# Layer norm of u: statistics merged on Pool, one ScalarE pass per row block, modulation of two row blocks per VectorE instruction

## The chip, the cores and the metric

The kernel runs on one core of a Trainium2 chip. The metric is the device time of one execution in microseconds (us), taken as the median of several executions. A core has five engines that each run their own instructions in order and wait for one another by semaphores: TensorE (PE in the profile, with PEld for its weight loads), VectorE (DVE), ScalarE (ACT), Pool (POOL, also called GpSimd) and SyncE (SP), which here only issues transfers. SBUF is the on-chip memory with 128 partitions; PSUM holds TensorE's results.

## What is computed

The reference is one transformer-like block over a sequence of 2048 positions with 512 channels: an adaptively modulated layer norm, a long convolution (S4), and then a second modulated layer norm with a mixer and an MLP. The part around the change is this:

```python
mod = (_silu(c) @ w_mod).reshape(c.shape[0], 6, 1, -1)
sa, ca, ga, sb, cb, gb = (mod[:, 0], ..., mod[:, 5])
h = _layernorm(x, axis=-1) * (1 + ca) + sa      # x is u: 2048 x 512
x = x + ga * _A_ref(h, ...)                     # S4: K = sum_n C exp(dt A l) dt B, FFT convolution of h with K
...
def _layernorm(x, axis=-1, eps=1e-5):
    m = jnp.mean(x, axis=axis, keepdims=True)
    v = jnp.var(x, axis=axis, keepdims=True)
    return (x - m) / jnp.sqrt(v + eps)
```

Each of the 2048 rows of u is normalised over its 512 channels, multiplied by (1 + ca) and shifted by sa; both are multiplied by ga ahead of time, since ga scales the whole branch. The result goes into the Fourier transform of u.

## The kernel before, in words

The program has stages. First come preparations (0 to 39 us of the trace): discretising A, B and C, and the first three parts of the modulation. Then comes the stage that matters here, the generation of the S4 kernel (about 39 to 212 us), a loop of 33 steps (line 553) written out by hand under a manual schedule: every engine runs its instructions in the order of the program text. After it come the two-dimensional spectra and their products (212 to 335 us) and the mixer with the MLP (335 to 715 us).

One step k of the loop issues, in this order:

- the evictions that the step before left in the list `later` (ScalarE): kernel blocks `KX<-kp` after every odd step, Fourier blocks of u `vs<-pu`, and at some steps parts of the modulation (`wm`, `modg`).
- `turns(k + 2)` (line 448): TensorE computes phases into PSUM (`xx`, two buffers), ScalarE takes a sine and a cosine of 128x1024 each into the tile `tr` (three buffers). So phases and sines are made two steps ahead of their use.
- at every fourth step (k = 1, 5, 9, 13, 17, 21, 25; `fresh`, line 561) the exponentials for the next four steps: `exps` (line 243) on TensorE and ScalarE. ScalarE then runs a table load for Exp, five Exp instructions `p<-xx`, and at the end, at line 579, a tiny sine `turn<-hpi` that brings the table load for Sin forward. These steps are called exponential steps below.
- `products(k)` (line 468) on VectorE: two scalar_tensor_tensor of 128x512 (L475), at even k one tensor_tensor of 128x1024 for two steps together (L481), and two tensor_tensor of 128x1024 (L484, L485). All read two tensors from SBUF and write the tiles `e0` and `e1`. In step 0 and at the end of every step with k % 4 == 3 a small `weigh` (L263) is added.
- `burst(k)` (line 499): 64 small matmuls on TensorE from `e0` and `e1`.
- the entries of `side[k]` (lines 515 to 533): the work on u and on the modulation, spread over the steps by a table.

The work on u has 16 row blocks of 128 rows (one row per partition) and 512 channels, four to a tile `xu`. For row block i the table uses at(i) = 1 + (i * 28) // 16, that is 1, 2, 4, 6, 8, 9, 11, 13, 15, 16, 18, 20, 22, 23, 25, 27:

- at side[at(i) - 2] `u_stats` (line 418, through `ln_stats`, line 141): VectorE's bn_stats (L146) and bn_aggr (L147) give mean and variance; Pool adds eps (L149) and takes the power -0.5 (L150).
- at side[at(i)] `u_norm` (line 421): two scalar_tensor_tensor of 128x512 on VectorE, in place: (x - mean) * mods[1] (L424), then x * rstd + mods[0] (L425).
- for every odd i, at side[at(i) + 1] and side[at(i) + 2], `u_dft` (line 427) for the pair of row blocks i - 1 and i: eight matmuls, and for the next step's evictions two ScalarE copies `vs<-pu` and four transfers out on SyncE's queue.

Pool's queue holds, beside these, the issues of eight DRAM-to-DRAM copies of the weights (L519, at side[4], side[7], ... side[25]).

Where the engine instructions stand in the loop, in the lines that matter most:

```python
fresh = k % 4 == 1 and k < 28
if fresh:
    exps(k // 4 + 1, 0, 2)
e = products(k)
...
    act(turn1, hpi, AF.Sin)
...
for f in side[k]:
    f()
```

So what `side[k]` puts on ScalarE in an exponential step stands behind all five Exp instructions and both table loads of that step.

Of the kernel before, what the change touches and what calls it, by code (L numbers as in the profile page):

```python
# [7 lines left out]
F32 = mybir.dt.float32  # L8
F32R = mybir.dt.float32r
I32 = mybir.dt.int32  # L10
AF = mybir.ActivationFunctionType
OP = mybir.AluOpType
# [94 lines left out]
def dram(t, off, ap):  # L107
    return bass.AP(tensor=t.tensor, offset=t.offset + off, ap=ap)


def body(ctx, tc, A):
    nc = tc.nc
    V, S, P, T, Y = nc.vector, nc.scalar, nc.gpsimd, nc.tensor, nc.sync
    pool = lambda name, bufs=1, **k: tc.tile_pool(name=name, bufs=bufs, **k)
    glob = ctx.enter_context(pool("glob"))
    dpool = ctx.enter_context(pool("dscr", space=DRAM))

    def act(out, in_, f=AF.Copy, scale=1.0, bias=0.0):
        return S.activation(out, in_, f, bias=bias, scale=scale)  # L119
# [11 lines left out]
    eps_t = glob.tile([128, 8], F32, name="eps_t")  # L131
    V.memset(eps_t, 1e-5)
    pw = glob.tile([128, 8], F32, name="pw")
    V.memset(pw, -0.5)
    m_one = glob.tile([128, 8], F32, name="m_one")
    V.memset(m_one, -1.0)
    mv1 = glob.tile([128, 16, 2], F32, name="mv1")
    rs1 = glob.tile([128, 16], F32, name="rs1")
    st1 = glob.tile([128, 10, 2, 6], F32, name="st1")

    def ln_stats(pl, xs, tag):
        n = len(xs)
        st = pl.tile([128, n, 6], F32, name=tag + "s")
        mv = pl.tile([128, n, 2], F32, name=tag + "m")
        for i, x in enumerate(xs):
            V.bn_stats(st[:, i], x)  # L146
            V.bn_aggr(mv[:, i], st[:, i])  # L147
        r = pl.tile([128, n], F32, name=tag + "r")
        P.tensor_tensor(r, mv[:, :, 1], eps_t[:, :n], op=OP.add)  # L149
        P.tensor_tensor(r, r, pw[:, :n], op=OP.pow)  # L150
        return mv, r

    def exp_exact(pl, x, shape, name, scale=1.0):
        t = lambda s, dt=F32: pl.tile(shape, dt, name=f"{name}_{s}")
# [47 lines left out]
    mods = [modu[:, k] for k in range(3)] + [modg[:, k] for k in range(3)]  # L202
# [29 lines left out]
    ut = {}  # L232

    def load_u(g):
        x = ut[g] = up.tile([128, 4, 512], F32, name="xu")
        for bp in range(4):
            Y.dma_start(x[bp * 32:(bp + 1) * 32],
                        dram(A["u"], (bp * 16 + g * 4) * 512, [[64 * 512, 32], [1, 2048]]))
# [45 lines left out]
    with tc.manual_schedule():  # L284
# [89 lines left out]
        at, at0 = tmp("at"), tmp("at0")  # L374
# [36 lines left out]
    wk = a1.enter_context(pool("wk", bufs=2, reuse_waits="tile"))  # L411
# [4 lines left out]
    ul = {}  # L416

    def u_stats(b):
        ul[b] = ln_stats(wk, [ut[b // 4][:, b % 4]], "lu")

    def u_norm(b):
        x = ut[b // 4][:, b % 4]
        mv, r = ul.pop(b)
        V.scalar_tensor_tensor(x, x, mv[:, 0, 0:1], mods[1], op0=OP.subtract, op1=OP.mult)  # L424
        V.scalar_tensor_tensor(x, x, r[:, 0:1], mods[0], op0=OP.mult, op1=OP.add)  # L425

    def u_dft(b, cp2):
        x = ut[b // 4]
        ps = [psu.tile([128, 512], F32, name="pu") for h in range(2)]
        for i in range(2):  # L430
            for h in range(2):
                q = 64 * (1 - i if h == 0 else i)
                j = slice(32 * JB[2 * h + cp2], 32 * JB[2 * h + cp2] + 32)
                T.matmul(ps[h][q:q + 64], FU[j, h, cp2 * 64:cp2 * 64 + 64], x[j, b % 4 + i],
                         start=True, stop=True, skip_group_check=True)

        def evict():
            vs = uv.tile([128, 2, 512], F32, name="vs")
            for h in range(2):
                act(vs[:, h], ps[h])  # L440
                c0 = h * 32 + cp2 * 16 + (14 - b if h == 0 else b)
                for i in range(2):
                    Y.dma_start(dram(VU, (c0 + i) * 256, [[16384, 64], [1048576, 2], [1, 256]]),
                                vs[i * 64:i * 64 + 64, h].rearrange("p (a d) -> p a d", a=2))
        later.append(evict)
# [69 lines left out]
    side = {k: [] for k in range(40)}  # L515
    for k in range(8):
        w, i = ("w3", k) if k < 4 else ("w4", k - 4)
        n = A[w].shape[0] // 4
        side[4 + 3 * k].append(lambda w=w, i=i * n, n=n: P.dma_start(WD[w][i:i + n], A[w][i:i + n]))  # L519
    for n in range(3, 6):  # L520
        k = 7 * n - 9
# [1 line left out]
        side[k].append(lambda n=n: later.append(mod_parts(n)))  # L523
        side[k + 1].append(lambda n=n: later.append(mod_sum(n)))
    at = lambda i: 1 + (i * 28) // 16
    for i in range(16):
        side[max(at(i) - 2, 0)].append(lambda i=i: u_stats(i))
        side[at(i)].append(lambda i=i: u_norm(i))
        if i % 2 == 1:
            side[at(i) + 1].append(lambda i=i: u_dft(i - 1, 0))  # L530
            side[at(i) + 2].append(lambda i=i: u_dft(i - 1, 1))
        if i % 4 == 3 and i < 8:
            side[at(i) + 2].append(lambda i=i: load_u(i // 4 + 2))

    def add_skip(h, g0, g1):
        V.tensor_add(Kq[:, h, g0:g1, 31], DS[:, h * 64 + g0:h * 64 + g1], Kq[:, h, g0:g1, 31])
# [546 lines left out]
    with tc.manual_schedule():  # L1083
# [12 lines left out]
        for n, st in enumerate(steps):  # L1096
            p = spectrum_k(*st)
# [126 lines left out]
        n = cm.tile([128, 2, 512], F32, name="h2")  # L1224
        sm = [(cm.tile([128, 2], F32, name="cmv"), cm.tile([128, 1], F32, name="crs")) for i in range(2)]
# [17 lines left out]
        r = transposed(n)  # L1243
        split_w(1)
        r = parts_of(r)
# [4 lines left out]
        for g in range(8):  # L1250
            r = chan(g, r)
# [18 lines left out]
```

## Time and profile before

| what | value |
|---|---|
| median of 3 runs | 718.54 us (714.7 to 720.83) |
| profiled execution | 716.82 us, its span 715.1 us |
| TensorE busy | 671.7 us, 94% of the span |
| VectorE busy | 506.3 us, 71% |
| ScalarE busy | 335.6 us, 47% |
| Pool busy | 85.6 us, 12% |

How to read it: the span is the profiled part of one execution, and the execution's time is 1.7 us longer. A timeline row gives the start and the duration in us, the engine, the line of the kernel, the operation, the output and inputs by their tile names with sizes, and how many instructions were merged into the row (x2); in brackets stands the idle time before it and what ended that. The durations of successive VectorE or ScalarE instructions overlap a little at their ends, so the cost of an instruction in a busy queue is the distance from its start to the next start. Line 119 is the helper through which all ScalarE instructions go, so there one goes by tile names. A step of the loop is recognised on VectorE by its L475 row (its first instruction; an even step goes on with L481) and on ScalarE by the `tr` rows.

### The profile page before, as it was taken

How to read it: one execution, taken by the hardware profiler on the slowest of the kernel's cores; microseconds unless marked ns; L12 is line 12 of the kernel's file. 1: busy time of each engine (PE TensorE's matmuls, PEld its weight loads, DVE VectorE, ACT ScalarE, POOL GpSimd, SP SyncE). 2: the span in 40 equal slices, each digit the busy share in tenths (PEclk: the TensorE clock that was granted, in tenths of full speed). 3: DMA queues.
4: the chain of work that ended last, by engine and by line, in shares of the span. 5: the costliest groups of instructions: out<-in, count | busy, mean ns of one | idle time of the engine just before them, and what ended most of it. 6: DMA issues, size and time to landing. Idle time of an engine off the chain costs nothing.

```text
span 715.1 us, 16869 instructions
## 1 busy us (share of the span) xinstructions
PE 671.7 (94%) x7083; PEld 520.1 (73%) x7083; DVE 506.3 (71%) x847; ACT 335.6 (47%) x549; POOL 85.6 (12%) x191
## 2 busy tenths in 40 slices
PE   2689999999999899998899999999999999999997
PEld 1356655666568566664688889989898998989896
DVE  8989999999986566767978868557463635454422
ACT  2768898889956255634245623313123121212121
POOL 1011212112000001100463200201010000000000
PEclk9999999999999999999999999999999999999999
DMA  8452274744439999793649402011020111111011
GB/s 286 152 129 69 74 217 102 191 128 116 132 80 266 232 289 315 224 324 144 217 149 302 132 5 56 15 45 31 16 74 16 49 27 31 31 30 30 0 30 31
DMA packets 56884, 85.52 MB, mean 120 GB/s; under 512 B 5764, under 2 KB 43656, under 8 KB 55144
## 3 DMA queue, kind: packets, MB, share of 16 engines
q1 hardware_dynamic: 52648, 66.61, 34.8%
q0 software_dynamic: 3136, 16.52, 6.4%
q10 hardware_dynamic: 1024, 1.31, 0.6%
q8 instruction: 56, 0.92, 0.5%
q14 instruction: 20, 0.16, 0.1%
HBM read 58.20 MB, written 31.85 MB: 126 GB/s over the span
## 4 chain that ended last, share of the span: by engine, by line
PE 48%; DVE 2%; ACT 1%; DMA 1%; SPq 0%; issue 0%; POOL 0%; DVEq 0%; ACTq 0%
PE pm L825 7%; PE pm L828 7%; PE pm L826 7%; PE pa L949 6%; PE pa L941 6%; PE pa L942 5%; PE ph L879 2%; PE ph L880 2%; PE ph L882 2%; PE pT L790 2%; DMA ld<-ZT 1%; PE pT L1140 1%; PE py L722 1%; ACT nh L119 0%; DVE st L758 0%; SPq L707 0%
## 5 line engine op out<-in xcount | busy, mean ns | idle before, releaser
L119 ACT ACTIVATE gh<-pm 128x512 fp32r<-128x512 f32 (+1 forms) x48 | 26.9, 560 | 200.7 <-PE pm L828 200.7
L825 PE MATMUL pm<-nh,w3h 128*128 128x256 f32 (+1 forms) x352 | 85.8, 279 | 0.9 <-ACT nh L119 0.9
L826 PE MATMUL pm<-nh,w3l 128*128 128x256 f32 (+1 forms) x352 | 85.6, 279 | 0.1
L933 DVE TENSOR_TENSOR gl<-gf,gh 128x512 fp32r<-128x512 f32 (+1 forms) x48 | 30.8, 642 | 68.4 <-ACT gf L119 68.4
L941 PE MATMUL pa<-w4h,gh 128*128 128x512 f32 (+1 forms) x176 | 69.6, 396 | 0.0
L942 PE MATMUL pa<-w4l,gh 128*128 128x512 f32 (+1 forms) x176 | 68.9, 392 | 0.0
L825 PEld LDWEIGHTS pm<-nh,w3h 128*128 128x128 f32 (+1 forms) x352 | 65.3, 185 | 2.6 <-ACT nh L119 1.1
L826 PEld LDWEIGHTS pm<-nh,w3l 128*128 128x128 f32 (+1 forms) x352 | 65.2, 185 | 2.2 <-DVE w3l L744 0.5
L828 PE MATMUL pm<-nl,w3h 128*128 128x256 f32 (+1 forms) x352 | 54.8, 277 | 0.0
L949 PE MATMUL pa<-w4h,gl 128*128 128x512 f32 (+1 forms) x176 | 48.1, 391 | 0.8 <-DVE gl L933 0.8
L458 PE MATMUL xx<-MG,ON 64*128 64x512 f32 x160 | 48.0, 396 | 0.0
L457 PE MATMUL xx<-MG,ON 64*128 64x512 f32 x160 | 48.0, 396 | 0.0
L828 PEld LDWEIGHTS pm<-nl,w3h 128*128 128x128 f32 (+1 forms) x352 | 46.7, 185 | 0.2 <-DVE nl L798 0.2
L753 POOL TENSOR_TENSOR rs<-mv,eps_t 128x1 f32<-128x1 f32 (+1 forms) x39 | 11.4, 293 | 279.0 <-DVE mv L759 266.6
L678 DVE TENSOR_TENSOR ma<-pk,us 128x512 f32<-128x512 f32 x32 | 21.9, 685 | 30.7 <-issue 22.9
L119 ACT ACTIVATE z<-pz 128x512 f32<-128x512 f32 x32 | 17.5, 595 | 54.6 <-PE pz L693 38.3
L885 DVE TENSOR_TENSOR h<-h,ph 128x512 f32<-128x512 f32 x16 | 11.0, 686 | 45.2 <-PE ph L882 45.2
L475 DVE SCALAR_TENSOR_TENSOR e<-tr,p 128x512 f32<-128x512 f32 x64 | 41.0, 682 | 2.1 <-ACT tr L119 1.9
L949 PEld LDWEIGHTS pa<-w4h,gl 128*128 128x128 f32 (+1 forms) x176 | 33.0, 188 | 8.3 <-DVE gl L933 1.2
L484 DVE TENSOR_TENSOR e<-tr,p 128x1024 f32<-128x1024 f32 x32 | 38.9, 1217 | 0.0
L507 PEld LDWEIGHTS kp<-e,e 128*32 128x32 f32 x2048 | 30.0, 110 | 12.2 <-issue 8.1
L485 DVE TENSOR_TENSOR e<-tr,m 128x1024 f32<-128x1024 f32 x32 | 38.9, 1216 | 0.0
(234 smaller groups left out, 1763.5 us busy)
## 6 DMA issues: line engine op xcount, KB each, us to landing
VU<-vs SPq DMA_DIRECT2D x64, 128.0 KB, 3.5
ld<-VU SPq DMA_DIRECT2D x32, 256.0 KB, 10.4
ZT<-z POOLq DMA_DIRECT2D x15, 512.0 KB, 8.3
ld<-ZT SPq DMA_DIRECT2D x12, 512.0 KB, 8.2
Dw<-in_w POOLq DMA_DIRECT2D x8, 688.0 KB, 4.7
xu<-in_u SPq DMA_DIRECT2D x16, 256.0 KB, 6.8
KX<-in_u SPq DMA_DIRECT2D x16, 256.0 KB, 10.2
GD<-go SPq DMA_DIRECT2D x16, 256.0 KB, 2.3
```

What stands on the lines that cost most here:

```text
L119: return S.activation(out, in_, f, bias=bias, scale=scale)
L457: T.matmul(x[:, :512], la, ma, start=(i == 0), stop=(i == len(ops) - 1))
L458: T.matmul(x[:, 512:], lb, mb, start=(i == 0), stop=(i == len(ops) - 1))
L475: V.scalar_tensor_tensor(e0[:, 1, a], tr[:, 1, 0], 1.0 - 2.0 * a, mg[:, a], op0=OP.mult, op1=OP.mult)
L484: V.tensor_mul(e0[:, 0], tr[:, 0, 0:1].to_broadcast([128, 2, 512]), mg)
L485: V.tensor_mul(e1.rearrange("p r d q -> p r (d q)"), tr[:, :, 1], m1s[0][:, u % 2:u % 2 + 1].to_broadcast([128, 2, 512]))
L825: T.matmul(p, wh[:, k, c], hi[k], start=(k == 0), stop=False)
L826: T.matmul(p, wl[:, k, c], hi[k], start=False, stop=False)
L828: T.matmul(p, wh[:, k, c], lo[k], start=False, stop=(k == 3))
L941: T.matmul(acc[i], gh[:m, e, s], W4h[:m, f], start=(f == 0), stop=False)
L942: T.matmul(acc[i], gh[:m, e, s], W4l[:m, f], start=False, stop=False)
L949: T.matmul(acc[i], gl[:m, e, s], W4h[:m, f], start=False, stop=(f == 10))
```

## The change

Row blocks are handled in pairs p = 0 to 7 (row blocks 2p and 2p + 1). `ln_stats` and `u_norm` are gone, and a tile of constants `lnc` is set at the start (five small memsets on VectorE).

- VectorE keeps bn_stats per row block, and bn_aggr is dropped. bn_stats leaves counts, means and scaled variances of the even and the odd elements.
- Pool merges the two halves for both row blocks of a pair at once: ten tensor_tensor instructions on 128x2x1 or 128x2x2 elements give the mean, the variance, its power -0.5 (r) and -mean * r, where there were four (two per row block).
- ScalarE normalises each row block by one Identity activation with scale r and bias -mean * r, in place (`u_scale`). This is new work for ScalarE.
- VectorE multiplies a pair by mods[1] and adds mods[0], each by one tensor_tensor of 128x1024 with the modulation broadcast over the two row blocks (`u_mod`).

With o = max(at(2p + 1), 3), that is 3, 6, 9, 13, 16, 20, 23, 27, the table becomes: bn_stats of the first row block at side[o - 4] (0 at least), bn_stats of the second and the Pool merge at side[o - 3], `u_scale` at side[o - 2], the multiplication at side[o - 1], the addition at side[o], the two halves of `u_dft` at side[o + 1] and side[o + 2], and the loads of later row blocks where they were. `u_dft` of the first pair moves one step later, all others stay.

```diff
+    lnc = glob.tile([128, 5], F32, name="lnc")
+    for i, v in enumerate((0.5, 1.0 / 512, 1e-5, -0.5, -1.0)):
+        V.memset(lnc[:, i:i + 1], v)
...
     def u_stats(b):
-        ul[b] = ln_stats(wk, [ut[b // 4][:, b % 4]], "lu")
-
-    def u_norm(b):
-        x = ut[b // 4][:, b % 4]
-        mv, r = ul.pop(b)
-        V.scalar_tensor_tensor(x, x, mv[:, 0, 0:1], mods[1], op0=OP.subtract, op1=OP.mult)
-        V.scalar_tensor_tensor(x, x, r[:, 0:1], mods[0], op0=OP.mult, op1=OP.add)
+        p, i = divmod(b, 2)
+        if i == 0:
+            ul[p] = [wk.tile([128, 2, n], F32, name=f"lu{n}") for n in (6, 2, 1, 3)]
+        st, sm, d, rn = ul[p]
+        V.bn_stats(st[:, i], ut[b // 4][:, b % 4])
+        if i == 1:
+            t = lambda o, x, y, op: P.tensor_tensor(o, x, y, op=op)
+            c = lambda q: lnc[:, None, q:q + 1].to_broadcast([128, 2, 1])
+            t(sm, st[:, :, 1:3], st[:, :, 4:6], OP.add)
+            t(sm, sm, lnc[:, None, 0:2].to_broadcast([128, 2, 2]), OP.mult)
+            t(d, st[:, :, 1:2], st[:, :, 4:5], OP.subtract)
+            t(d, d, c(0), OP.mult)
+            t(d, d, d, OP.mult)
+            t(rn[:, :, 0:1], sm[:, :, 1:2], d, OP.add)
+            t(rn[:, :, 0:1], rn[:, :, 0:1], c(2), OP.add)
+            t(rn[:, :, 0:1], rn[:, :, 0:1], c(3), OP.pow)
+            t(rn[:, :, 2:3], sm[:, :, 0:1], c(4), OP.mult)
+            t(rn[:, :, 1:2], rn[:, :, 2:3], rn[:, :, 0:1], OP.mult)
+
+    def u_scale(p):
+        rn = ul.pop(p)[3]
+        for i in range(2):
+            x = ut[p // 2][:, p % 2 * 2 + i]
+            act(x, x, AF.Identity, scale=rn[:, i, 0:1], bias=rn[:, i, 1:2])
+
+    def u_mod(p, k, op):
+        x = ut[p // 2][:, p % 2 * 2:p % 2 * 2 + 2]
+        V.tensor_tensor(x, x, mods[k][:, None].to_broadcast([128, 2, 512]), op=op)
...
-    for i in range(16):
-        side[max(at(i) - 2, 0)].append(lambda i=i: u_stats(i))
-        side[at(i)].append(lambda i=i: u_norm(i))
-        if i % 2 == 1:
-            side[at(i) + 1].append(lambda i=i: u_dft(i - 1, 0))
-            side[at(i) + 2].append(lambda i=i: u_dft(i - 1, 1))
-        if i % 4 == 3 and i < 8:
-            side[at(i) + 2].append(lambda i=i: load_u(i // 4 + 2))
+    for p in range(8):
+        o = max(at(2 * p + 1), 3)
+        side[max(o - 4, 0)].append(lambda p=p: u_stats(2 * p))
+        side[o - 3].append(lambda p=p: u_stats(2 * p + 1))
+        side[o - 2].append(lambda p=p: u_scale(p))
+        side[o - 1].append(lambda p=p: u_mod(p, 1, OP.mult))
+        side[o].append(lambda p=p: u_mod(p, 0, OP.add))
+        side[o + 1].append(lambda p=p: u_dft(2 * p, 0))
+        side[o + 2].append(lambda p=p: u_dft(2 * p, 1))
+        if p in (1, 3):
+            side[o + 2].append(lambda p=p: load_u(p // 2 + 2))
```

More of the change, by code (lines that the diff above doesn't have):

```diff
@@ L139, in body @@
     st1 = glob.tile([128, 10, 2, 6], F32, name="st1")
[L141 to L151, printed above, removed]
     def exp_exact(pl, x, shape, name, scale=1.0):
```

## The prediction

> **What bounds the kernel now.** I read the page first, then busy time by windows, then the timelines of VectorE, ScalarE and Pool inside the stage that the change touches (about 39 to 212 us). The windows from step 3 to step 27 and behind the stage:
>
> ```profile
> PE 671.7 (94%) x7083; PEld 520.1 (73%) x7083; DVE 506.3 (71%) x847; ACT 335.6 (47%) x549; POOL 85.6 (12%) x191
> ```
>
> ```profile
> core 0: us, PE busy (x) PEld busy (x) DVE busy (x) ACT busy (x) POOL busy (x), PEclk, DMA share, GB/s
> 59.57:189.17 129.60, 125.79 (x2176) 78.84 (x2173) 127.59 (x167) 114.59 (x137) 24.49 (x36) 0.99 0.51 139
> 212.84:715.10 502.26, 483.93 (x4118) 404.41 (x4116) 303.64 (x546) 165.83 (x344) 55.72 (x141) 0.99 0.39 111
> ```
>
> VectorE is busy 127.59 of 129.60 us: the stage runs at VectorE's pace. But ScalarE is busy 88% of it as well, so the stage has little ScalarE to spare. Behind the stage TensorE is busy 96% and nothing of it touches u's row blocks, so I let a shift of the stage's end pass to the end one for one. VectorE's timeline around steps 4 and 5:
>
> ```profile
> 66.85 1.22 DVE L485 TENSOR_TENSOR e<-tr,m 128x1024 f32<-128x1024 f32 x1
> 67.98 0.74 DVE L424 SCALAR_TENSOR_TENSOR xu<-xu,lum,modu 128x512 f32<-128x512 f32 x1
> 68.84 0.75 DVE L425 SCALAR_TENSOR_TENSOR xu<-xu,lur,modu 128x512 f32<-128x512 f32 x1
> 69.51 0.69 DVE L146 BATCH_NORM_STATS2 lus<-xu 128x6 f32<-128x512 f32 x1
> 70.23 0.18 DVE L147 BATCH_NORM_AGGREGATE lum<-lus 128x2 f32<-128x6 f32 x1
> 70.33 1.28 DVE L475 SCALAR_TENSOR_TENSOR e<-tr,p 128x512 f32<-128x512 f32 x2
> 71.53 1.22 DVE L484 TENSOR_TENSOR e<-tr,p 128x1024 f32<-128x1024 f32 x1
> 72.67 1.22 DVE L485 TENSOR_TENSOR e<-tr,m 128x1024 f32<-128x1024 f32 x1
> 73.80 0.68 DVE L475 SCALAR_TENSOR_TENSOR e<-tr,p 128x512 f32<-128x512 f32 x1
> ```
>
> From start to start, one row block of u costs 70.33 - 67.98 = 2.35 us, a 128x1024 tensor_tensor 1.13, a 128x512 instruction that waits for nothing 0.60 (two in 1.20), an odd step 73.80 - 70.33 = 3.47, an even one 3.47 + 1.13 = 4.60.
>
> **VectorE's work.** Removed: 16 x 2.35 = 37.6 us. Added: per pair two bn_stats, no longer followed by a dependent bn_aggr, at 0.60 as above, and two 128x1024 tensor_tensor at 1.13: 3.46, times 8 = 27.7. Saved: 9.9 us. The five memsets of the constants are priced at nothing (0.2 us at most, 128 elements or fewer being far below any row above).
>
> **ScalarE's work.** Two passes per pair. The nearest row is the same form in the mixer:
>
> ```profile
> 358.54 1.51 ACT L119 ACTIVATE h<-h,nm,rs 128x512 f32<-128x512 f32 x2
> ```
>
> ```profile
> 159.59 0.60 ACT L119 ACTIVATE modg<-pu 128x512 f32<-128x512 f32 x1 [0.96 <-PE pu L227]
> 160.77 1.03 ACT L119 ACTIVATE tr<-xx 128x1024 f32<-128x1024 f32 x1 [0.58 <-PE xx L458]
> ```
>
> So 1.51 us a pair, 12 us in all; seven pairs would raise the 114.59 above to about 125 of 129.6. No table load comes with it: the modulation's fifth part is an Identity too (159.59), and the sine behind it follows without a load.
>
> **What is queued behind the new waits.** VectorE's multiplication at side[o - 1] now waits for ScalarE, and ScalarE's passes at side[o - 2] wait for Pool. Behind the multiplication stand VectorE's products of all later steps, for which TensorE's bursts wait; behind the passes stand ScalarE's evictions and the sines of step o + 1. So the question is where each queue stands when VectorE arrives. For three pairs (p = 0, 6, 7) o - 2 is 1, 21, 25: exponential steps. There the passes stand behind the whole exponential work:
>
> ```profile
> 182.40 1.03 ACT L119 ACTIVATE tr<-xx 128x1024 f32<-128x1024 f32 x1
> ...
> 184.62 1.28 ACT L119 ACT_TABLE_LOAD   x1
> 185.91 4.90 ACT L119 ACTIVATE p<-xx 128x1024 f32<-128x1024 f32 x5
> 190.83 1.28 ACT L119 ACT_TABLE_LOAD   x1
> ...
> 192.23 0.58 ACT L119 ACTIVATE KX<-kp 128x512 f32<-128x512 f32 x1
> ```
>
> ```profile
> 178.75 1.28 DVE L475 SCALAR_TENSOR_TENSOR e<-tr,p 128x512 f32<-128x512 f32 x2
> ...
> 189.17 1.28 DVE L475 SCALAR_TENSOR_TENSOR e<-tr,p 128x512 f32<-128x512 f32 x2
> ```
>
> VectorE's products of step 24 end at 178.75. ScalarE is through with step 25's exponentials only at 192.23, where VectorE is nearly through with step 27. The multiplication of p = 7 is due after step 26: at 178.75 + 0.60 (statistics) + 3.47 + 4.60 = 187.4. ScalarE delivers at 192.23 + 1.51 + 0.1 = 193.8. Wait: 6.4 us. The same two readings for the other two:
>
> ```profile
> 155.22 0.74 DVE L424 SCALAR_TENSOR_TENSOR xu<-xu,lum,modu 128x512 f32<-128x512 f32 x1
> ```
>
> ```profile
> 170.62 0.58 ACT L119 ACTIVATE KX<-kp 128x512 f32<-128x512 f32 x1
> ```
>
> ```profile
> 44.81 0.69 DVE L146 BATCH_NORM_STATS2 lus<-xu 128x6 f32<-128x512 f32 x1
> ```
>
> ```profile
> 60.84 0.58 ACT L119 ACTIVATE KX<-kp 128x512 f32<-128x512 f32 x1
> ```
>
> p = 6: due at 155.22 + 1.13 + 0.60 + 3.47 + 4.60 = 165.0, delivered at 170.62 + 1.61 = 172.2: 7.2 us. Here ScalarE needs 15.4 us from the end of step 20's products, against 13.5 at p = 7, because older work is still queued there; a later VectorE lets it clear that, so I take 13.5, and 5.3 us. p = 0: due at 44.81 + 1.20 + 3.47 + 1.20 (two products of modulation parts) + 4.60 = 55.3, delivered at 62.45: 7.2 us. Sum of the three: 18.9. This can't be hidden: each wait holds the products of the next step.
>
> The other five pairs wait less. For p = 4 and 5 (o - 2 = 14 and 18) the passes come one step behind exponentials, after that step's sines; the eviction `vs` that follows these marks the place:
>
> ```profile
> 118.52 1.28 DVE L475 SCALAR_TENSOR_TENSOR e<-tr,p 128x512 f32<-128x512 f32 x2
> ...
> 139.69 1.28 DVE L475 SCALAR_TENSOR_TENSOR e<-tr,p 128x512 f32<-128x512 f32 x2
> ```
>
> ```profile
> 129.53 1.11 ACT L119 ACTIVATE vs<-pu 128x512 f32<-128x512 f32 x2
> ...
> 151.44 1.11 ACT L119 ACTIVATE vs<-pu 128x512 f32<-128x512 f32 x2
> ```
>
> Steps 14 and 18 start on VectorE at 118.52 and 139.69; the multiplication is due 4.60 + 3.47 + 0.33 (weigh) = 8.4 later, at 126.9 and 148.1; ScalarE delivers at 129.53 + 1.61 = 131.1 and 153.1. Waits of 4.2 and 5.0. ScalarE was idle 15 us in the 129.6, about 2.5 in each of the six intervals between exponential steps, and can turn that into lead while VectorE waits: 1.8 and 2.6. I take 3.0 each, between the two.
>
> For p = 1, 2, 3 ScalarE is in time, and Pool's chain of ten sets the end.
>
> ```profile
> 45.80 0.19 POOL L149 TENSOR_TENSOR lur<-lum,eps_t 128x1 f32<-128x1 f32 x1 [36.69 <-DVE lum L147]
> 46.07 0.57 POOL L150 TENSOR_TENSOR lur<-lur,pw 128x1 f32<-128x1 f32 x1
> ```
>
> ```profile
> 70.51 0.55 POOL L149 TENSOR_TENSOR lur<-lum,eps_t 128x1 f32<-128x1 f32 x1 [8.72 <-DVE lum L147]
> 71.14 0.90 POOL L150 TENSOR_TENSOR lur<-lur,pw 128x1 f32<-128x1 f32 x1
> ```
>
> ```profile
> 375.00 0.74 DVE L765 SCALAR_TENSOR_TENSOR h<-h,rs,modg 128x512 f32<-128x512 f32 x1
> ```
>
> ```profile
> 375.38 0.42 POOL L814 TENSOR_TENSOR nm<-mv,m_one 128x1 f32<-128x1 f32 x1
> ```
>
> At 45.80 VectorE runs bn_stats, with one input, and Pool's addition takes 0.19. At 70.51 it runs L475, with two inputs from SBUF, and the same addition takes 0.55: it ends at 71.06, which is 0.19 after the end of that L475's reading (70.33 + 0.54). The power that follows ends 0.57 after the second L475. At 375.38 only the rest of the L765 is waited out, and the time is 0.42. So a Pool instruction starts when the VectorE instruction in front of it ends, and Pool gets one instruction through per VectorE instruction. Ten of them take the nine or ten VectorE instructions of steps o - 2 and o - 1: the result is there about 8.5 us after step o - 2 begins, ScalarE delivers at 10.1, and VectorE is due at 8.07 or (with a weigh) 8.40. Waits: 2.0 + 1.7 + 1.7 = 5.4. Bounds: uncontended, ten instructions at 0.27 take 3 us, and the wait is 0. [...] The rows agree with blocking to the instruction's end; if the delay were a constant 0.36 per instruction instead, the chain would take 6.9 us and p = 1 to 3 would wait 0.1 to 0.4 each, some 5 us less in the sum. VectorE itself loses nothing to Pool in these rows (two L475 take 1.20 with Pool running beside them).
>
> **The sum.** Against the profiled execution's 716.8 us (its span of 715.1 and 1.7 around it, and 1.7 below the median of the runs): -9.9 (work) + 18.9 (p = 0, 6, 7) + 6.0 (p = 4, 5) + 5.4 (p = 1 to 3) = +20.4, so 737 us. Low end: p = 1 to 3 nothing, p = 4 and 5 4.4, the other three 2.4 less each (11.7): +6.2, 723. High end: 20.8 + 9.2 + 5.4 - 9.9 = +25.5, and 4 us for the spread of the runs: 746.
>
> **Rivals.**
>
> 1. Faster: ScalarE's order does not bind, VectorE saves its 9.9 us: 707 us. It needs the passes done before VectorE's second step ends, 8.1 us after step o - 2 begins. For it: VectorE is the stage's fullest engine. Against it: the 192.23 and 170.62 above. [...]
> 2. No change: ScalarE catches up further than I allow, and the waits come to about 10 us, what the work saves: 717 us. For it: ScalarE alone, at 125 of 129.6 us, would fit. Against it: that leaves it 4%, and the three exponential pairs alone wait more.
> 3. Much slower: Pool gets through only once per two VectorE instructions, since ten in a row from 128x2 elements are not the pairs seen here. Half the chain is left when VectorE arrives, five instructions at 0.27 and a power, 1.7 us, and with the passes held as long the sines come late too: two and a half us more in each of p = 1 to 5, 750 us.
>
> **How the numbers follow.** The forecast 737 us has 0.72, rival 1 0.08, rival 2 0.10, rival 3 0.10. The range 722 to 746 is the forecast's own; rivals 1 and 3 and part of 2 lie outside, about 2 in 10. Within 1%, 711 to 726, about what a measurement of this kernel can tell from no change, lie rival 2 and the forecast's low edge, 0.03: 0.13 same, 0.08 faster, 0.79 slower.
>
> **What would show it.** In the changed profile VectorE should sit idle in front of the two-row-block multiplication, released by ScalarE, some 5 to 7 us each before steps 3, 23 and 27 and 1 to 4 us in the other pairs; ScalarE's `xu` passes should follow directly on `turn` in three pairs; Pool's small instructions should last 0.2 to 1.1 us each, ending at VectorE's boundaries; the first spectra instructions should start near 232 us instead of 212. If VectorE stays over 97% busy from step 3 to 27, the prediction is wrong.

## The result and the profile after

The changed kernel takes 754.5 us (median of 4 runs, 747.01 to 755.71) against 717.9 for the kernel before, run beside it: 1.0495 times as long, 95% interval 1.0451 to 1.0539. The direction was forecast, the size was not: 737 us, 722 to 746. One of the four runs took 747.0, at a granted TensorE clock of 0.984 against 0.967 to 0.971 in the others; its trace was not kept, so which wait it was spared is not known. The profiled execution took 753.83 us with a span of 752.1. Lines of the changed kernel behind the work on u stand 12 to 15 further down, those between the dropped `ln_stats` and the work on u 9 further up (`exps`' matmuls L247, `weigh` L254): the products' first line is L487, the row statistics L414, Pool's merge L416, the two-row-block instruction L437, the bursts L519, `vs`'s source L446.

The page's busy times of the changed kernel: VectorE did 6 us less, ScalarE 9 us more, Pool 52 us more.

```profile
PE 693.2 (92%) x7083; PEld 531.6 (71%) x7083; DVE 500.3 (67%) x820; ACT 345.0 (46%) x565; POOL 138.1 (18%) x239
```

Windows over the whole stage, from VectorE's first product to the last addition of the skip (L536 before, L551 after). First the kernel before:

```profile
39.28:212.84 173.56, 166.96 (x2894) 104.76 (x2895) 169.09 (x220) 147.44 (x176) 26.64 (x40) 0.99 0.46 120
```

The same windows of the changed kernel, and all that lies behind:

```profile
40.95:251.67 210.72, 184.49 (x2898) 113.62 (x2895) 162.66 (x188) 156.87 (x192) 78.38 (x88) 0.91 0.36 98
251.67:752.10 500.43, 486.24 (x4118) 406.27 (x4117) 304.09 (x546) 165.80 (x344) 56.36 (x141) 1.00 0.37 111
```

The stage grew by 37.2 us; it started 1.7 later and what lies behind it took 1.8 less (502.26 before). So everything is in the stage, and the whole difference of the spans, 37.0, with it. VectorE was idle for 4.5 us of it before and is for 48.1 now. Its waits, in the view of waits from 40 to 256 us of the changed kernel (total, times, longest):

```profile
DVE xu L437 <- ACT xu L119: 37.2, 7, 8.9
DVE e L487 <- PE kp L519: 6.6, 1, 6.6
DVE e L487 <- ACT tr L119: 4.0, 2, 3.1
```

The first row is the one that was forecast, with 30.3. The second was in no term of the sum. Of the third, 3.1 us lie ahead of the stage's first product; in the stage there are 0.9, and 1.2 more for `p`. Together with the 9.9 us of work saved: -9.9 + 37.2 + 6.6 + 2.1 = 36.0 of the 37.2; the rest is in shorter waits.

Now one pair, p = 1. VectorE's timeline in the changed kernel (start, duration, what it waited for in brackets):

```profile
71.03 0.69 DVE L414 BATCH_NORM_STATS2 lu<-xu 128x6 f32<-128x512 f32 x1
71.63 1.28 DVE L487 SCALAR_TENSOR_TENSOR e<-tr,p 128x512 f32<-128x512 f32 x2
...
78.56 1.22 DVE L497 TENSOR_TENSOR e<-tr,m 128x1024 f32<-128x1024 f32 x1
84.15 1.23 DVE L437 TENSOR_TENSOR xu<-xu,modu 128x1024 f32<-128x1024 f32 x1 [4.37 <-ACT xu L119]
```

Pool's timeline at the same place:

```profile
71.79 8.05 POOL L416 TENSOR_TENSOR lu<-lu 128x4 f32<-128x4 f32 x1 [15.46 <-DVE lu L414]
79.92 0.20 POOL L416 TENSOR_TENSOR lu<-lu,lnc 128x4 f32<-128x4 f32 x1
...
80.89 0.20 POOL L416 TENSOR_TENSOR lu<-lu,lu 128x2 f32<-128x2 f32 x1
```

By the prediction the first addition should have ended at the first boundary between two VectorE instructions, at 72.2. It lasted 8.05 us, through nine VectorE instructions with two inputs from SBUF, and ended when VectorE had nothing left to do (78.56 + 1.22 = 79.78). With VectorE idle the others take 0.2 us each, the power some 0.6. So here Pool's chain went through only while VectorE waited for it. In the other pairs the first addition took 0.56 (p = 0), 3.43, 3.77, 8.38, 8.38, 8.04 and 8.04 us; wherever it lasted 3 us or more, it ended as VectorE ran out of work. The eight additions make 48.7 of the 52 us by which Pool is busier. Below, the addition is called let in when it ends at VectorE's first or second boundary, and shut out when it lasts longer. ScalarE stood waiting for it, in its timeline of the changed kernel:

```profile
82.60 1.52 ACT L119 ACTIVATE xu<-xu,lu 128x512 f32<-128x512 f32 x2 [8.38 <-POOL lu L416]
...
219.63 4.89 ACT L119 ACTIVATE p<-xx 128x1024 f32<-128x1024 f32 x5
224.54 1.28 ACT L119 ACT_TABLE_LOAD   x1
225.83 0.20 ACT L119 ACTIVATE turn<-hpi 128x1 f32<-128x1 f32 x1
225.94 1.50 ACT L119 ACTIVATE xu<-xu,lu 128x512 f32<-128x512 f32 x2
```

The last four rows are p = 7: the passes right behind the exponentials, as forecast. TensorE, meanwhile, stood idle in front of its bursts and came out of it at a lower granted clock. Its timeline (idle time in brackets), and the windows around the first of these places (the third figure from the right is the granted clock), both of the changed kernel:

```profile
76.37 1.94 PE L519 MATMUL kp<-e,e 128*32 128x64 f32 x64 [3.29 <-DVE e L497]
86.05 2.22 PE L247 MATMUL xx<-CE,TES 32*128 32x512 f32 x4 [2.24 <-ACT tr L119]
```

```profile
72.00:76.00 4.00, 1.07 (x10) 0.56 (x6) 4.00 (x5) 2.14 (x2) 4.00 (x1) 1.00 0.00 0
76.00:80.00 4.00, 3.63 (x72) 2.00 (x72) 3.79 (x5) 0.00 (x0) 3.92 (x2) 0.53 0.01 4
```

The clock was 0.50 to 0.81 from 76 to 104 us, over the exponentials of step 5 and the sines behind them, and at the end of it VectorE waited for a burst to free its buffer, as its timeline shows:

```profile
103.97 1.29 DVE L487 SCALAR_TENSOR_TENSOR e<-tr,p 128x512 f32<-128x512 f32 x2 [6.56 <-PE kp L519]
```

### The profile page after: what moved, and what is told of

Same layout as the page of the kernel before. It is cut to its first block, busy times and chain, and to the rows that moved or that the text cites. A ratio compares the mean times of both kernels' runs of the same rounds, so it can differ in the third digit from the quotient of the medians.

```text
span 752.1 us, 16897 instructions
## 1 busy us (share of the span) xinstructions
PE 693.2 (92%) x7083; PEld 531.6 (71%) x7083; DVE 500.3 (67%) x820; ACT 345.0 (46%) x565; POOL 138.1 (18%) x239
## 4 chain that ended last, share of the span: by engine, by line
PE 47%; DVE 2%; DMA 1%; ACT 1%; issue 0%; POOL 0%; SPq 0%; DVEq 0%; ACTq 0%
PE pm L843 7%; PE pm L840 7%; PE pm L841 7%; PE pa L964 5%; PE pa L957 5%; PE pa L956 5%; PE ph L894 2%; PE ph L897 2%; PE ph L895 2%; PE pT L805 2%; PE py L737 1%; PE pT L1155 1%; DMA ld<-ZT 1%; PE pm L737 0%; DVE st L773 0%
## 5 line engine op out<-in xcount | busy, mean ns | idle before, releaser
L841 PE MATMUL pm<-nh,w3l 128*128 128x256 f32 (+1 forms) x352 | 87.3, 281 | 0.1
L416 POOL TENSOR_TENSOR lu<-lu 128x2 f32<-128x2 f32 (+1 forms) x32 | 56.4, 1764 | 131.1 <-DVE lu L414 129.8
L843 PE MATMUL pm<-nl,w3h 128*128 128x256 f32 (+1 forms) x352 | 56.5, 282 | 0.0
L519 PEld LDWEIGHTS kp<-e,e 128*32 128x32 f32 x2048 | 33.7, 119 | 27.0 <-DVE e L497 18.8
L519 PE MATMUL kp<-e,e 128*32 128x64 f32 x2048 | 39.2, 235 | 13.8 <-DVE e L497 13.8
L470 PE MATMUL xx<-MG,ON 64*128 64x512 f32 x160 | 50.1, 411 | 0.0
L469 PE MATMUL xx<-MG,ON 64*128 64x512 f32 x160 | 50.1, 410 | 0.0
L487 DVE SCALAR_TENSOR_TENSOR e<-tr,p 128x512 f32<-128x512 f32 x64 | 41.1, 684 | 10.5 <-PE kp L519 6.6
L437 DVE TENSOR_TENSOR xu<-xu,modu 128x1024 f32<-128x1024 f32 x16 | 19.6, 1222 | 37.3 <-ACT xu L119 37.2
L119 ACT ACTIVATE p<-xx 128x1024 f32<-128x1024 f32 (+1 forms) x40 | 37.6, 980 | 6.3 <-PE xx L247 4.6
```

What stands on the lines that cost most here:

```text
L416: t = lambda o, x, y, op: P.tensor_tensor(o, x, y, op=op)
L469: T.matmul(x[:, :512], la, ma, start=(i == 0), stop=(i == len(ops) - 1))
L470: T.matmul(x[:, 512:], lb, mb, start=(i == 0), stop=(i == len(ops) - 1))
L487: V.scalar_tensor_tensor(e0[:, 1, a], tr[:, 1, 0], 1.0 - 2.0 * a, mg[:, a], op0=OP.mult, op1=OP.mult)
L519: T.matmul(kp[32 * j:32 * j + 32, (k % 2) * 4 + g], e1[:, r, d], e0[:, r, :, d * 32:d * 32 + 32], start=(r == 0), stop=(r == 1), skip_grou ...
L841: T.matmul(p, wl[:, k, c], hi[k], start=False, stop=False)
```

## The experiments

Four theories. **A**: ScalarE's queue; the passes stand behind other work and VectorE's multiplication comes too early for them. **B**: Pool's first addition is shut out by VectorE's two-input instructions. **C**: the idle stretches take TensorE's clock down, and that costs on its own. **D**: what lets Pool in is a short gap in VectorE's row of instructions. The ratios are against the kernel before, run beside them. In `e7_bubble`, `e8_nodep`, `e11_ahead` and `e12_spread` VectorE computes one small result per pair that nothing uses; in `e3_fill` and `e10_front_fill` TensorE does.

**The multiplication one step later.**

```
-        side[o - 1].append(lambda p=p: u_mod(p, 1, OP.mult))
+        side[o].append(lambda p=p: u_mod(p, 1, OP.mult))
```

> The multiplication moves from side[o - 1] to side[o], right ahead of the addition; all else as in the changed kernel. Theory A (ScalarE's queue is late by a fixed time, VectorE's multiplication comes one step too early): every wait in front of the multiplication shrinks by one step of VectorE (3.5 to 4.6 us, 3.8 with a weigh), so 6.9, 4.4, 0, 1.6, 4.5, 4.4, 6.4, 8.9 us become about 3.1, 0, 0, 0, 0, 0, 2.6, 5.1: 37 us become 11, and the kernel takes about 728 us. Theory B (Pool's first addition is shut out for as long as VectorE runs instructions with two inputs from SBUF back to back, and only VectorE's going idle lets it in): the first addition lasts one step longer, 11 to 13 us instead of 8, and each of pairs 1 and 3 to 7 still waits about 4 us for the other nine operations and ScalarE's passes: the waits stay near 30 us and the kernel near 748 us.

Measured: 731.4 us, 1.0212 (1.0151 to 1.0273). Waits and Pool's first additions of p = 1 and p = 7 in this kernel:

```profile
DVE xu L437 <- ACT xu L119: 9.0, 3, 4.1
DVE e L487 <- PE kp L519: 6.5, 1, 6.5
```

```profile
67.14 0.57 POOL L416 TENSOR_TENSOR lu<-lu 128x4 f32<-128x4 f32 x1 [15.22 <-DVE lu L414]
...
191.34 11.51 POOL L416 TENSOR_TENSOR lu<-lu 128x4 f32<-128x4 f32 x1 [13.38 <-DVE lu L414]
```

The waits for the passes fall from 37.2 to 9.0: 2.5, 2.4 and 4.1 in pairs 0, 6 and 7, theory A's numbers to within 1 us. Theory B is not refuted: in p = 3, 5 and 7 the addition was shut out for 3.77, 8.37 and 11.51 us, the last of them to the end of three steps' products; in p = 1, 2, 4 and 6 it got in at the first boundary, where it had not in the changed kernel. There the bn_stats now follows directly on multiplication and addition, of which the second must wait for the first (side by side in `e12_spread` it starts 1.26 us behind it, at 98.25 and 99.51; a product starts 1.13 behind another).

**bn_aggr back on VectorE, four operations on Pool instead of ten.**

```
         V.bn_stats(st[:, i], ut[b // 4][:, b % 4])
+        V.bn_aggr(mv[:, i], st[:, i])
         if i == 1:
...
+            t(rn[:, :, 0:1], mv[:, :, 1:2], c(2), OP.add)
+            t(rn[:, :, 0:1], rn[:, :, 0:1], c(3), OP.pow)
+            t(rn[:, :, 2:3], mv[:, :, 0:1], c(4), OP.mult)
+            t(rn[:, :, 1:2], rn[:, :, 2:3], rn[:, :, 0:1], OP.mult)
```

> Each row block gets its bn_aggr on VectorE back (0.1 us each from start to start, some 2 us in all), and Pool's chain has four operations of 128x2 instead of ten that begin with two of 128x4; the order of all else is that of the changed kernel. Theory B, in the form that the 128x4 operations do not fit at a boundary between two VectorE instructions while 128x2 ones do: the first Pool operation takes about 0.55 us, the chain about 5 us, the waits of pairs 1 to 5 (14.9 us) fall to 3 or less, those of pairs 0, 6 and 7 stay (22 us), and the kernel takes about 741 us. Theory A (ScalarE's order alone): pairs 4 and 5 keep their 4.5 us each, only pairs 1 and 3 gain (6 us), 750 us. If any first Pool operation is shut out, whatever its size: it still lasts 8 us, 750 to 753 us.

Measured: 745.5 us, 1.0398 (1.0320 to 1.0475), between the two. Pool was let in at once in all eight pairs. The waits for passes in its view of waits:

```profile
DVE xu L432 <- ACT xu L119: 28.9, 7, 8.8
```

Pairs 1 to 5 wait 0, 0.34, 0.95, 3.17 and 2.65 us, 7.1 instead of 14.9; pairs 4 and 5 keep most of theirs, which is theory A's part. The wait for `kp` is gone although the clock fell here too (0.50 from 76 to 80 us), for less long.

**More matmuls where TensorE stood idle.**

```
+        for _ in range({4: 10, 20: 7, 24: 10}.get(k, 0)):
+            T.matmul(kp.rearrange("p a b -> p (a b)"), TES[:, 0], CE[:, :512], start=True, stop=True,
+                     skip_group_check=True)
```

> TensorE gets 10, 7 and 10 more matmuls of 128x512 (0.23 us each) ahead of the bursts of steps 4, 20 and 24, where it stood idle for 3.3, 2.2 and 3.3 us before its granted clock fell; they write PSUM that the burst overwrites, so nothing of the result changes. Theory C (the idle stretch takes the clock down, and TensorE at half clock then holds the others): the clock is 1.0 from 76 to 104 us and from 208 to 216, the 6.6 us that VectorE waits for kp go, and the kernel takes 742 to 746 us. If the falls of the clock have another cause: they stay, and the kernel stays at 754 us.

Measured: 751.5 us, 1.0501 (1.0440 to 1.0562), no different from the changed kernel. Its windows at the first and the third place, its wait in front of p = 7, and TensorE's next idle stretch:

```profile
76.00:80.00 4.00, 4.00 (x84) 2.45 (x72) 3.11 (x4) 0.00 (x0) 3.77 (x5) 1.00 0.00 0
80.00:84.00 4.00, 0.07 (x2) 0.00 (x0) 0.53 (x1) 2.08 (x4) 2.09 (x7) 0.77 0.52 176
...
212.00:216.00 4.00, 3.52 (x74) 2.12 (x72) 4.00 (x5) 3.89 (x5) 4.00 (x1) 1.00 0.54 120
```

```profile
222.43 1.23 DVE L437 TENSOR_TENSOR xu<-xu,modu 128x1024 f32<-128x1024 f32 x1 [6.09 <-ACT xu L119]
```

```profile
85.37 2.22 PE L247 MATMUL xx<-CE,TES 32*128 32x512 f32 x4 [5.30 <-ACT tr L119]
```

Where the idle stretch was filled, the clock stayed: at 76, at 180 and at 212 us. The exponentials of step 25 were then in time, and the wait of p = 7 fell from 8.9 to 6.1 us (forecast: 6.4), that of p = 6 from 6.4 to 5.0 (forecast: 5.3). At the first place TensorE was done earlier and then stood idle 5.3 us for ScalarE's sine, the clock fell after all (0.77 from 80 to 84 us), and the 6.5 us for `kp` stayed. So TensorE at full clock does shorten the waits for passes, as C says, but little beside what makes TensorE idle. The stage is 3.5 us shorter than in the changed kernel; what lies behind it took 504.2 us in this execution against 500.4 there, so the whole time does not show it.

**The two 128x4 operations split into 128x2**, and so the two scalings.

```
-            t(sm, st[:, :, 1:3], st[:, :, 4:6], OP.add)
+            for q in range(2):
+                t(sm[:, :, q:q + 1], st[:, :, q + 1:q + 2], st[:, :, q + 4:q + 5], OP.add)
```

> The two 128x4 operations at the head of Pool's chain become four of 128x2, and nothing else changes. Theory B by size (a 128x4 operation does not fit at a boundary between VectorE instructions, a 128x2 one does): the first addition takes 0.5 to 0.7 us in every pair instead of 3.4 to 8.4, and the twelve operations end one per VectorE boundary, 10 to 12 us after the bn_stats, so the waits hardly shrink: 748 to 755 us. If any first operation after bn_stats is shut out: it still lasts 8 us, and the time stays at 754 us.

Measured: 755.2 us, 1.0570 (1.0493 to 1.0646). Pool's first two additions of p = 1, together:

```profile
70.27 8.20 POOL L416 TENSOR_TENSOR lu<-lu 128x2 f32<-128x2 f32 x2 [14.01 <-DVE lu L414]
```

A 128x2 operation is shut out like a 128x4 one: B's form "by size" is wrong. This kernel also qualifies `e3_fill`. At the second of theory C's places it has the idle stretch of the changed kernel and no matmul put in, and yet TensorE ran its burst at full clock (1.0 from 180 to 184 us, 0.75 in the changed kernel). The burst in the changed kernel, then in this one:

```profile
182.30 1.94 PE L519 MATMUL kp<-e,e 128*32 128x64 f32 x64 [2.16 <-DVE e L497]
```

```profile
181.00 1.10 PE L521 MATMUL kp<-e,e 128*32 128x64 f32 x64 [2.15 <-DVE e L499]
```

Its wait of p = 6 is 5.0 us, as in `e3_fill`: so 1.4 us there is the price of the half clock, but that the filling kept the clock is shown only at the first and the third place, where this kernel's clock fell.

**One bn_aggr between bn_stats and the products**, with Pool's ten operations kept; once of the row block just read (VectorE has to wait for it: such a bn_aggr starts 0.72 us behind its bn_stats in the kernel before, at 69.51 and 70.23), once of the other one, `st[:, 0]` (nothing to wait for: 0.61 us in `e8_nodep`, at 70.74 and 71.35).

```
+        if i == 1:
+            V.bn_aggr(wk.tile([128, 2], F32, name="lua"), st[:, 1])
```

> The changed kernel with one bn_aggr of the second row block behind its bn_stats, whose result nothing uses (0.1 us, but VectorE must finish the bn_stats before it: a short gap in its row of instructions). Pool's ten operations are those of the changed kernel. Theory D (Pool's operation is let in at the boundaries after VectorE has had such a gap, whatever the operation's size; e2_aggr and the kernel before have this gap by their bn_aggr): the first addition takes 0.5 to 0.7 us in every pair, the chain goes one per boundary and ends 8 to 10 us after the bn_stats, and the kernel takes 742 to 750 us. If the short chain of e2_aggr was let in for its own form: the first addition still lasts 8 us, 755 us.

> As e7_bubble, but the bn_aggr reads the first row block's statistics, done a step earlier, so that VectorE has nothing to wait for and no gap. Theory D: the first addition is shut out as in the changed kernel (3.4 to 8.4 us in pairs 1 to 7). If it is the bn_aggr as such (one short instruction with one input) that lets Pool in: 0.5 to 0.7 us as in e7_bubble.

Measured: 747.4 us, 1.0422 (1.0382 to 1.0461), and 747.1 in the one run of the second. Pool's timeline of p = 1 and the waits in `e7_bubble`, then Pool's first addition in `e8_nodep`:

```profile
73.13 0.20 POOL L417 TENSOR_TENSOR lu<-lu 128x4 f32<-128x4 f32 x1 [20.14 <-DVE lu L414]
73.41 0.52 POOL L417 TENSOR_TENSOR lu<-lu,lnc 128x4 f32<-128x4 f32 x1
...
80.35 1.05 POOL L417 TENSOR_TENSOR lu<-lu 128x2 f32<-128x2 f32 x1
```

```profile
DVE xu L438 <- ACT xu L119: 29.7, 8, 9.0
```

```profile
71.51 0.64 POOL L417 TENSOR_TENSOR lu<-lu 128x4 f32<-128x4 f32 x1 [20.11 <-DVE lu L414]
```

In both kernels the first addition took 0.19 to 0.64 us in all eight pairs, and the others then went one per VectorE boundary; the chain took 8.3 us (73.13 to 81.40), where 8.5 was forecast. So the gap is not needed, and theory D falls: a bn_aggr between bn_stats and the products does it. Whether that is because it is short or because it has one input was not tested. This kernel is the one that the prediction had in mind, and its waits for the passes are 29.7 us against 30.3 forecast. The stage is 9.4 us shorter than in the changed kernel (201.27 against 210.72): that is the price of the shut-out: 7.5 us in front of the multiplication and 6.6 at `kp`, less some 5 us for later sines, the last eviction and the added bn_aggr itself. (The intervals of the two ratios overlap a little, one run of the changed kernel was as short as this one, and the stages are of one execution each.)

**The same short instruction ahead of bn_stats.**

```
+        if i == 1:
+            V.bn_aggr(wk.tile([128, 2], F32, name="lua"), st[:, 0])
         V.bn_stats(st[:, i], ut[b // 4][:, b % 4])
```

> The changed kernel with one bn_aggr of the first row block's statistics (done a step earlier, result unused) ahead of the second bn_stats instead of behind it as in e8_nodep. [...] If it must stand between bn_stats and the two-input instructions: 3.4 to 8.4 us in pairs 1 to 7, as in the changed kernel.

Measured: 755.0 us in one run. Pool's first additions of p = 1 and p = 2:

```profile
73.26 8.05 POOL L418 TENSOR_TENSOR lu<-lu 128x4 f32<-128x4 f32 x1 [20.17 <-DVE lu L416]
...
93.94 0.56 POOL L418 TENSOR_TENSOR lu<-lu 128x4 f32<-128x4 f32 x1 [9.39 <-DVE lu L416]
```

0.56 us in pairs 0, 2 and 5, 3.77 to 8.38 in the five others: pairs 2 and 5 are let in, where all of 1 to 7 were to be shut out, and the others show that a short instruction ahead of bn_stats is not enough. What lets the first operation in when no short instruction stands between stays open.

**The passes of pairs 0, 6 and 7 in front of the exponentials; then the multiplication late as well; then late without the first.** All three have the short chain of `e2_aggr`; `front` holds steps 1, 21 and 25, in the first two kernels.

```
+                if k in front:
+                    u_scale(front[k])
                 if fresh:
                     exps(k // 4 + 1, 0, 2)
```

> The short chain of e2_aggr, and for pairs 0, 6 and 7 ScalarE's two passes stand in front of the exponentials of their step (1, 21, 25) instead of behind them. Theory A (these three waits come from the order on ScalarE alone): the three waits of 6.6, 6.4 and 8.8 us in e2_aggr go to nearly nothing, and some 7 us in pairs 2 to 5 stay: about 724 us. Rival (ScalarE has no room: what stands in front delays the exponentials and the sines behind them by as much, and VectorE then waits for p or tr): at most half of the 22 us comes back, 734 us or more.

> e5_front, and the multiplication moved to side[o] as in e1_mul_late. Theory A: no wait for ScalarE's passes is left, and what remains is the work that the change saves on VectorE (9.9 us less some 2 us for the bn_aggr that came back): about 708 us, faster than before. Rival (ScalarE is the bound of the stage with its 12 us of passes more): the waits turn up at tr, 714 us or more.

> The two edits of e1_mul_late and e2_aggr together: the multiplication at side[o] and the short chain on Pool; ScalarE's passes of pairs 0, 6 and 7 stay behind the exponentials. If Pool's lateness and ScalarE's order add up: pairs 1 to 5 wait for nothing, pairs 0, 6 and 7 keep 2.5, 2.5 and 5 us, and the half clock with its 6.5 us for kp goes as in e2_aggr: about 724 us. If what e2_aggr gained is the same time that e1_mul_late gained: no better than 731 us.

Measured: 731.6 us, 1.0205 (1.0163 to 1.0246); 725.9, 1.0118 (1.0080 to 1.0155); 722.9, 1.0081 (1.0051 to 1.0111). Waits of `e5_front`, then of `e6_front_late`, then of `e9_late_aggr`:

```profile
DVE e L482 <- ACT tr L119: 8.3, 6, 2.9
DVE xu L432 <- ACT xu L119: 7.2, 4, 3.2
DVE e L482 <- PE kp L514: 5.0, 1, 5.0
```

```profile
DVE e L482 <- PE kp L514: 4.4, 2, 4.1
DVE e L482 <- ACT tr L119: 4.0, 4, 1.6
...
DVE p L254 <- ACT p L119: 2.7, 3, 1.9
```

```profile
DVE xu L432 <- ACT xu L119: 5.8, 3, 2.1
DVE e L482 <- ACT tr L119: 5.7, 4, 3.1
```

(2.9 us of the first kernel's sines and 3.1 of the last one's lie ahead of the stage's first product.) In front of the exponentials the passes cost VectorE nothing: 28.9 us become 7.2. But `kp` takes 5.0, and of the 22 us 14 come back. With the multiplication late as well no wait for a pass is left, and theory A's 708 us are still missed by 18: 11 us of waits for sines, exponentials and bursts stand in their place, and VectorE saves 4.9 us instead of about 8 (u's instructions take 32.9 us from start to start: each bn_stats is followed by a bn_aggr that must wait for it, 0.72 us from start to start where 0.60 is without a wait, and multiplication and addition stand side by side, 2.40 us for the two in `e9_late_aggr` where two products take 2.27). Leaving the passes behind the exponentials does no worse (the intervals overlap): 5.8 us for the passes, 2.6 for sines in the stage, no fall of the clock (0.995 in the mean), no wait for `kp`.

**Matmuls among the first exponentials of steps 1, 21 and 25**, in `e6_front_late`; each `fill_half(6)` is six matmuls into the half of `kp` that the step's burst will overwrite.

```
-                    exps(k // 4 + 1, 0, 2)
+                    exps(k // 4 + 1, 0, 1)
+                    fill_half(pad)
+                    exps(k // 4 + 1, 1, 2)
+                    fill_half(pad)
```

> e6_front_late with twelve more matmuls of 128x256 (0.12 us each at full clock) among the first exponential matmuls of steps 1, 21 and 25, where TensorE stood idle 1.1 us at a time before its clock fell to 0.50 (168 to 174 and 192 to 202 us); they write PSUM that the burst of the step overwrites. Theory C (the idle stretches take the clock down, and TensorE at half clock holds VectorE): the clock stays at 1.0 there, the waits of 4.1 us for kp and 1.9 us for p go, and the kernel takes 720 to 722 us against 726. If the clock falls for another reason, or TensorE is late without it: 726 us or more.

Measured: 728.4 us, 1.0163 (1.0121 to 1.0205). From its view of waits:

```profile
DVE e L482 <- PE kp L519: 7.1, 1, 7.1
```

Around step 21 the clock stayed at 1.0 from 164 to 176 us, where `e6_front_late` had 0.73 and 0.84 from 168 to 176. At step 25 it fell at 188 us all the same, to 0.50: TensorE had been busy 2.33 of the 4 us before, ahead of the matmuls put in. The fill there stands behind the fall; whether the wait for `kp` is the clock's or the order's stays open here.

**Everything spread out:** the ten operations with the let-in of `e8_nodep`, passes one step later, multiplication and addition two steps after them, the transforms one later (pair 1 has its statistics a step earlier instead).

```
+        d = p != 1
+        side[max(o - 5 + d, 0)].append(lambda p=p: u_stats(2 * p))
+        side[o - 4 + d].append(lambda p=p: u_stats(2 * p + 1))
+        side[o - 2 + d].append(lambda p=p: u_scale(p))
+        side[o + d].append(lambda p=p: u_mod(p, 1, OP.mult))
+        side[o + d].append(lambda p=p: u_mod(p, 0, OP.add))
```

> An attempt at a version without the waits: Pool's ten operations of the changed kernel with the let-in of e8_nodep (one bn_aggr whose result nothing uses), ScalarE's passes at side[o - 1], none of them in an exponential step (for pair 1, whose o - 1 is one, statistics a step earlier and passes at side[o - 2] = 4), multiplication and addition both at side[o + 1] (pair 1: side[o]), transforms one step later as well. If what was found adds up (one Pool operation per VectorE boundary, passes behind each other's steps, multiplication two steps after the passes): no wait for the passes; VectorE keeps about 8 us of the 9.9 it saves, sines that are late by ScalarE's 12 us of added work take some 3 to 5 of it: 712 to 716 us against 717, just faster or the same. If ScalarE's added work is the bound whatever the order, or the half clock comes back: 720 us or more, as in e9_late_aggr.

Measured: 726.6 us, 1.0170 (1.0127 to 1.0213). From its view of waits:

```profile
DVE e L488 <- ACT tr L119: 12.8, 8, 3.0
DVE e L488 <- PE kp L520: 5.0, 3, 1.9
```

No wait for a pass, but 11 us for sines in the stage (1.8 of the first row lie ahead of it) and 5 for bursts. No order tried brings the change below the kernel before.

The stage in all kernels, with VectorE's idle times in it added up by what ended them (from its timelines, in us):

| kernel | stage | for passes | for sines and p | for kp | ratio |
|---|---|---|---|---|---|
| before | 173.6 | - | 0 | 0 | 1 |
| changed | 210.7 | 37.2 | 2.1 | 6.6 | 1.0495 |
| e4_split | 210.7 | 36.6 | 2.1 | 6.2 | 1.0570 |
| e11_ahead | 207.7 | 35.7 | 5.7 | 0 | - |
| e3_fill | 207.2 | 32.9 | 2.1 | 6.5 | 1.0501 |
| e8_nodep | 200.9 | 30.6 | 4.3 | 0 | - |
| e7_bubble | 201.3 | 29.7 | 4.1 | 0 | 1.0422 |
| e2_aggr | 200.2 | 28.9 | 3.2 | 0 | 1.0398 |
| e1_mul_late | 188.6 | 9.0 | 7.7 | 6.5 | 1.0212 |
| e5_front | 187.3 | 7.2 | 6.6 | 5.0 | 1.0205 |
| e10_front_fill | 183.9 | 0 | 7.2 | 7.1 | 1.0163 |
| e12_spread | 183.9 | 0 | 12.1 | 5.0 | 1.0170 |
| e6_front_late | 180.5 | 0 | 6.7 | 4.4 | 1.0118 |
| e9_late_aggr | 177.3 | 5.8 | 2.6 | 0 | 1.0081 |

What lies behind the stage took 500.4 to 505.0 us in these traces, with no relation to the stage, so differences of a few us between whole times of single runs say nothing. In each of the seven kernels with a wait of 4 us or more for a burst, that wait ends within 2 us of the end of a stretch of half clock (in the changed kernel, of the stretch from 86 to 104 us). But `e7_bubble` had half clock from 77 to 86 us and no such wait, and no run holds the order and changes the clock alone at such a place: that the half clock makes these waits is argued.

## Why the prediction was wrong in size

- **VectorE's work** was right: u's instructions took 37.8 us from start to start in the kernel before and 27.8 in the changed one, 9.9 saved.
- **ScalarE's two passes** were right: 1.5 us a pair, no added table load.
- **Stage to end one for one** was right to within a few us: 500.4 us behind the stage against 502.3 before, and no more than 505.0 in any kernel.
- **The failed step** is "Pool gets one instruction through per VectorE instruction". It was read off one-element operations that each stood behind a bn_aggr. The change takes the bn_aggr away, and without it the first operation was shut out for 3.4 to 8.4 us in seven pairs of eight. The waits for the passes were forecast as 7.2, 2.0, 1.7, 1.7, 3.0, 3.0, 5.3 and 6.4 us and came out as 6.9, 4.4, 0, 1.6, 4.5, 4.4, 6.4 and 8.9; with the bn_aggr put back (`e7_bubble`) they are 6.9, 1.6, 0.3, 0.9, 3.4, 2.7, 4.8 and 9.0, in sum the forecast. (Not one by one: p = 7 waits 2.6 us longer than forecast, and p = 2 and 3 some 2 us less together; that these cancel is luck.) Rival 3 had Pool late, at half the rate; it was not a rate, but all or nothing.
- **A term that was missing:** the sum had VectorE wait for the passes alone. TensorE's idle stretches and half clock (6.6 us for `kp`) and late sines and exponentials (2.1) were in none. In `e7_bubble`, where Pool works as forecast, the stage still grows by 27.7 us instead of 20.4: late sines (4.1), the last eviction (2.7 against 1.5) and its added bn_aggr (1.7). So with the Pool step alone put right the kernel takes 747 and not 737, still outside the range: of the 16.8 us by which the stage missed, 9.4 are the shut-out with what follows from it.
- The miss is 37.0 - 20.4 = 16.6 us: 6.9 in front of the multiplication, 6.6 for `kp`, 2.1 for sines and `p`, the rest in shorter waits.
- **ScalarE's order** was the right main cause: with the passes of three pairs put in front of the exponentials (`e5_front`), the waits for passes fell from 28.9 to 7.2 us. (One step more for the multiplication took 28 of the 37 us away, but that gives Pool time as well.) But rival 1, "VectorE saves its 9.9 us" once the order does not bind, was out of reach in every order tried: in the three kernels without any wait for a pass 11 to 17 us of other waits stand there. ScalarE's 12 us more, on an engine that was 88% busy, come back as late sines and bursts wherever the passes are put. This last is argued from the table; no kernel took other work off ScalarE to show it.
- **Two readings** were off without moving a term. The 0.54 us that an L475 is said to read for stands in no row (it is the difference of a 128x1024 and a 128x512 instruction, 1.22 - 0.68), and no row shows a reading that ends before its instruction; by the rows the first one ends at 71.01 (70.33 + 0.68), the addition beside it at 71.06, and the power ends 0.43 after the second one, not 0.57. And with 0.36 us more for each of ten instructions the chain of 3 us would take 6.6, not 6.9.

## What to carry to other kernels

Work taken from a full engine to one that is 88% busy and works in order is worth only what the second engine's queue leaves: read from the timeline what stands in front of the moved instruction and when its result is due. A helper engine's small operations must be priced beside the very instructions that will run next to them: with the short instruction that used to stand there taken away, the price went from 0.55 us to 8.05 here. And where a wait makes TensorE idle, a lower clock can follow: in the changed kernel it was 0.53 behind 3.29 us, and the burst took 1.94 us instead of 1.10.

## What the runs showed of the hardware

- Pool's first addition of p = 1, 0.20 us in `e7_bubble`, took 8.05 us in the changed kernel beside nine VectorE instructions that each read two inputs from SBUF; the longest, 11.51 us (`e1_mul_late`, p = 7), lasted to the end of the row of products. With a bn_aggr between bn_stats and the products it was let in at once in every pair of three kernels (0.19 to 0.64 us in `e7_bubble` and `e8_nodep`), and later operations went one per boundary (1.06 us each in `e7_bubble`, 1.13 or 1.14 from start to start). So a Pool addition can stay shut out over one VectorE instruction after another; by what, no run shows. VectorE lost nothing: its 128x1024 products took 1.21 to 1.23 us in the changed kernel, 1.21 or 1.22 in the kernel before.
- TensorE's granted clock fell to 0.53 behind an idle stretch of 3.29 us and stayed at 1.0 where that was filled with ten matmuls (`e3_fill`). But no length of idle time divides falls from others in these traces: behind 2.16 us it fell in the changed kernel and behind 2.15 it did not in `e4_split`; behind 3.38 us in `e11_ahead` it did not either; and in the kernel before it fell at 80 us, with TensorE busy for 3.84 of the 4 us ahead. TensorE's timeline and the window behind it in `e11_ahead`, then the window of the kernel before:

```profile
77.84 1.10 PE L521 MATMUL kp<-e,e 128*32 128x64 f32 x64 [3.38 <-DVE e L499]
```

```profile
80.00:84.00 4.00, 2.22 (x18) 1.50 (x18) 1.26 (x2) 0.00 (x0) 3.45 (x11) 1.00 0.00 0
```

```profile
80.00:84.00 4.00, 3.82 (x18) 2.64 (x18) 3.97 (x7) 3.71 (x6) 1.98 (x3) 0.57 0.33 110
```

What makes the clock fall, these runs do not show.
